# Linear attention and a one-expert mixture on one core: VectorE's order within a block, the release of the row scatter, and the second expert's first loads

## The chip, the core and the metric

The kernel runs on one core of a Trainium2 chip. The metric is the device time of one execution in microseconds (us). The kernel before took 397.58 us in the median of three runs (396.27, 397.58 and 398.49). The profile shown here is of one further execution, which took 397.19 us.

## The reference

Two parts run one after the other. The attention part is a linear recurrence with a decay, over 4 batches, 8 heads, 768 steps and 48 channels; its output is the input of a mixture of 8 experts, in which every one of the 3072 tokens goes to the one expert with the largest logit.

```
for t in range(S):
    cur = einsum('bhd,bhe->bhde', u * k[t], v[t])
    y[t] = einsum('bhd,bhde->bhe', r[t], state + cur)
    state = w[t][..., None] * state + einsum('bhd,bhe->bhde', k[t], v[t])
x = y.transpose(0, 2, 1, 3).reshape(3072, 384)
idx = argmax(x @ w_gate);  gate = softmax(x @ w_gate)[idx]
out[idx == e] = gate * (relu(x[idx == e] @ w1[e]) @ w2[e])
```

## The kernel before

**Attention.** The sequence is cut into 12 chunks of 64 steps, and each chunk into two blocks (two of the four batches each), so there are 24 blocks, numbered n. A call `iteration(n)` holds work of several blocks, since the stages are staggered by hand. The order in which the calls stand in the code is the order on each engine: the lists of TensorE, VectorE, ScalarE, GpSimd and SyncE are written out by hand, and each engine takes its own list in order.

In `iteration(n)` VectorE has: the running product of the decays from the left for block n+2 (`dve_pre`, a scan, and a short reciprocal), the same from the right for block n+1 (`dve_suf`, a scan, L360), the keys of block n+1 times that product (`dve_kh`, L368), and the masked copy of block n (`dve_at`, L373): the scores that TensorE has left in `ap` are copied into `at` where a mask allows. In one iteration of four VectorE also takes the choice of the expert (`gate`) for a group of four blocks, in the next one the place of each row (`place`).

TensorE has in `iteration(n)`: the transposes of the rows of block n-1 (`pe_xT`), the share of the old state (`pe_inter`, L481), the scores from `kh` and `rh` (`pe_a`, L466), the bonus and the transposes of the keys (`pe_kt`), the scores times the values (`pe_av`, L491, which reads `at`), and the state's update (`pe_dp`, L501).

GpSimd has: `rh` (receptance times left product, L395), `rk` (receptance times keys of block n+2, L387), one indirect DMA that scatters 128 finished rows into a table by expert (L604; it is held back until `pe_av(n)`), a tiny memset, and half of the diagonal of `at` (L423). Before `rk`, GpSimd waits for the `kh` of the same iteration, through a dependency added by hand:

```
i = nc.gpsimd.tensor_tensor(out=d["rk"], in0=d["r"], in1=d["k"], op=ALU.mult)
if n > 1:
    after(i, ch["kh"], "one port")
```

SyncE loads the blocks six ahead (L101, L104, L115). All loads of the kernel are issued on SyncE's one queue, in the order of the code.

**From attention to experts.** After the last block the rows of the largest expert (chosen in iteration 18, from the counts so far) are worked on in two portions: `ua` (256 rows, loaded early) and `ub_` (208 rows, loaded when the last scatters have landed). The last eight scatters go out one after the other on GpSimd; the first of them waits for the copy `act_xT(z)` of the last block. `side()` takes one piece of a weight at a time and splits it into a high half (ScalarE, L237) and a low half (VectorE, L239); when a staged piece is used up, `feed()` loads the next one if its expert's number is known. The numbers of experts 2 to 8 in the order of size come from `sort_experts()`; they are read into SyncE's registers (`expert_of`) in one run of seven, behind the load of `ub_`.

**Experts.** For each expert, `mm1` computes eight slabs of the first product (`expand`, L311), the results are split again into two halves (L313, L314), and `contract` or its transposed form makes the second product (L325, L975). TensorE runs nearly without a gap here.

Of the kernel before, what the change touches and what calls it, by code (L numbers as in the profile page):

```python
# [13 lines left out]
ALU = mybir.AluOpType  # L14
# [18 lines left out]
GRP = 4  # L33
# [22 lines left out]
def rwkv_moe_kernel(ctx, tc, rkw, vv, ub, wg, wr, w1, w2, out):  # L56
# [307 lines left out]
    def dve_kh(n):  # L364
        if real(n):
            d = blk[n]
            d["kh"] = work([RP, NSEG, C], F32, "kh")
            ch["kh"] = nc.vector.tensor_tensor(out=d["kh"], in0=d["k"], in1=d["suf"][:, :, 3:SEG], op=ALU.mult)  # L368

    def dve_at(n):  # L370
        if real(n):
# [11 lines left out]
    def pool_rk(n):  # L383
        if real(n):
            d = blk[n]
            d["rk"] = work([RP, NSEG, C], F32, "rk")
            i = nc.gpsimd.tensor_tensor(out=d["rk"], in0=d["r"], in1=d["k"], op=ALU.mult)  # L387
            if n > 1:
                after(i, ch["kh"], "one port")

    def pool_rh(n):
        if real(n):
# [61 lines left out]
    def act_xT(n):  # L454
        if real(n):
            blk[n]["xT"] = t = xtp.tile([P, DM], F32, name="xT", tag="xT")
            ch["xt"] = nc.scalar.activation(t, blk[n]["xp"], AF.Copy)

    def pe_a(n):
        if real(n):  # L460
# [70 lines left out]
    def logit_mm(k):  # L531
        G, at, m = k
        lp = misc("lp")[0:32 * m, 0:P]
        for j in range(3):
            for i in range(m):
                nc.tensor.matmul(lp[32 * i:32 * i + 32], wgt[:, j, :], blk[G * GRP + at + i]["xT"][:, j * P:(j + 1) * P],
                                 start=(j == 0), stop=(j == 2))
        ch["ls"] = ls = sm.tile([P, P], F32, name="ls", tag="ls")[0:32 * m]
        nc.scalar.activation(ls, lp, AF.Copy)

    def logit_tr(k):
        lt = misc("lt")[:, 0:32 * k[2]]
# [161 lines left out]
    def iteration(n):  # L704
        G, i = divmod(n, GRP)
        g = G - 1 if n >= 0 else -1
        whole = (g, 0, GRP)
        if 0 <= n < E // 2:
            prefill(2 * n)
            prefill(2 * n + 1)  # L710
        if n >= 0:
            load(n + 6)
        full = 0 <= g < NG - 1
        if real(n):
            blk[n]["ap"] = psA.tile([P, 4, 256], F32, name="ap", tag="ap")
            pe_xT(n - 1, blk[n]["ap"][:, 1:3, :].rearrange("p a c -> p (a c)"))
            pe_inter(n)
            if full and i == 1:
                logit_tr(whole)
            pe_a(n)  # L720
        dve_scale(n + 1)
        if full and i == 2:
            place(whole)
        act_pend(n + 1)
        act_g(n + 1)
        pool_rh(n + 1)
        dve_suf(n + 1)
        if n == -2:
            pool_rk(0)
        pe_kt(n)  # L730
        act_pad(n + 2)
        dve_kh(n + 1)
        if full and i == 1:
            gate(whole)
        dve_at(n)
        if n == NB - 2:
            side()
        act_kt(n)
        act_ct(n + 1)
        if n > -2:  # L740
            pool_rk(n + 2)
        pe_av(n)
        if n < 2:
            act_diag(n + 1, range(0, H if n < 0 else NQ))
        if n == NB - 2:
            dve_diag(n + 1)
            act_xT(n - 1)
            act_xr(n)
        else:
            act_xr(n)  # L750
            act_xT(n - 1)
        if 2 <= n < NB - 2:
            act_diag(n + 1, range(0, NQ))
        if moved(n) and n < NB - 2:
            scatter(*moved(n), ch["av"])
        if n >= 0:
            pool_diag(n + 1)
        dve_pre(n + 2)
        pe_dp(n)
        if n >= 0:  # L760
            load_v(n + LV)
        if n == FIRST * GRP + 6:
            choose()
            eid[0] = expert_of(first[0:1, 0:1])
            feed()
        if full and i == 0:
            logit_mm(whole)
        if full and i == 1:
            weigh(whole)
            pool_ids(g)  # L770
            rank(whole)
        if n == 3:
            late_constants()
# [65 lines left out]
    with tc.manual_schedule(engines={ET.PE, ET.DVE, ET.Activation, ET.Pool}):  # L839
# [16 lines left out]
        pool_ids(last)  # L856
        pe_av(z)
        logit_mm(ka)
        act_xr(z)
        transpose_rows(ua, 0)  # L860
        pe_xT(z, psA.tile([P, 4, 256], F32, name="xc", tag="ap")[:, 0:2, :].rearrange("p a c -> p (a c)"))
        act_xT(z)
        scatter(last - 1, range(GRP), ch["xt"])
        transpose_rows(ua, 1)
        logit_tr(ka)
        gate(ka)
# [7 lines left out]
        def mm1(u, f):  # L874
            expand(wts[u["e"] % 2], f, u["x"], u["n"], u["hs"])
# [10 lines left out]
        weigh(kb)  # L886
        place(kb)
        scatter(last, (3,))
        mm1(ua, 1)
        side(0)  # L890
        sort_experts()
        check_counts()
        for f in range(2, 8):
            mm1(ua, f)
            side(0)
        actx.close()
        wpb = mctx.enter_context(tc.tile_pool(name="wpb", bufs=1))
        wts.append(weight_tiles(wpb))
# [1 line left out]
        bk["b"].append(mM)  # L900
        while sides and sides[0][1] == 0:
            side(0)
        ub_ = rows_of(HB, HA, 0)
        for e in range(1, E):
            eid[e] = expert_of(order[0:1, e - 1:e])
        feed()
        un = rows_of(CAPS[1], 0, 1)
        tr = [(ub_, j) for j in range(3)]

        def tick():  # L910
# [18 lines left out]
        for e in range(1, E):  # L929
            u = un  # L930
            nth["e"] = e
            while tr:
                trans(*tr.pop(0))
            while sides and sides[0][0] == "split" and sides[0][1] == e:
                side()
            un = rows_of(CAPS[e + 1], 0, e + 1) if e + 1 < E else None
# [258 lines left out]
```

## Time and profile before

| | value |
|---|---|
| median of three runs | 397.58 us |
| the profiled execution | 397.19 us |
| its span (first to last instruction) | 395.5 us |
| around the span | 1.7 us |
| granted TensorE clock, mean | 0.973 |
| busy: TensorE, VectorE, ScalarE, GpSimd | 361.2, 264.2, 195.5, 145.1 us |
| chain that ended last, by engine | TensorE 74%, VectorE 9%, DMA 5%, ScalarE 5%, issue 4% |

A table by stage (the views give the numbers): the attention blocks fill the time up to about 139 us, the change-over some 10 us more, and the experts the rest. "Granted clock" is the share of TensorE's full clock that it was given: 1.00 is 2.4 GHz, 0.50 is 1.2 GHz. In a timeline each line is one group of instructions with start, duration, engine, line of code, operation and the names that it writes and reads; the bracket at its end is the idle time of its engine just before, and what ended it.

### The profile page before, as it was taken

How to read it: one execution, taken by the hardware profiler on the slowest of the kernel's cores; microseconds unless marked ns; L12 is line 12 of the kernel's file. 1: busy time of each engine (PE TensorE's matmuls, PEld its weight loads, DVE VectorE, ACT ScalarE, POOL GpSimd, SP SyncE). 2: the span in 40 equal slices, each digit the busy share in tenths (PEclk: the TensorE clock that was granted, in tenths of full speed). 3: DMA queues.
4: the chain of work that ended last, by engine and by line, in shares of the span. 5: the costliest groups of instructions: out<-in, count | busy, mean ns of one | idle time of the engine just before them, and what ended most of it. 6: DMA issues, size and time to landing. Idle time of an engine off the chain costs nothing.

```text
span 395.5 us, 11603 instructions
## 1 busy us (share of the span) xinstructions
PE 361.2 (91%) x4642; PEld 327.5 (83%) x4642; DVE 264.2 (67%) x451; ACT 195.5 (49%) x516; POOL 145.1 (37%) x195
## 2 busy tenths in 40 slices
PE   7889989797888978989999999999999999999991
PEld 5667767686666757879899899999999999999990
DVE  7788788998989757657565366466476576782410
ACT  4557546655555554445554355464465463761200
POOL 5757477667767728110200040040050171114010
PEclk9699989999999999999999999999999999999998
DMA  7996687777647415398833736466565756821001
GB/s 202 242 257 198 176 256 225 203 211 224 199 120 210 156 43 187 107 295 281 241 110 135 201 97 227 118 188 220 167 181 174 213 120 204 256 78 35 23 19 40
DMA packets 38021, 67.63 MB, mean 171 GB/s; under 512 B 8141, under 2 KB 19714, under 8 KB 37962
## 3 DMA queue, kind: packets, MB, share of 16 engines
q1 hardware_dynamic: 31658, 57.33, 49.5%
q0 software_dynamic: 6304, 9.50, 7.7%
q8 instruction: 38, 0.62, 0.7%
q14 instruction: 21, 0.17, 0.2%
HBM read 55.34 MB, written 11.64 MB: 169 GB/s over the span
## 4 chain that ended last, share of the span: by engine, by line
PE 74%; DVE 9%; DMA 5%; ACT 5%; issue 4%; SPq 1%; POOL 1%; POOLq 0%; DVEq 0%; ACTq 0%
PE N L311 12%; PE N L325 12%; PE cell L311 6%; PE N L975 6%; PE mM L311 6%; PE yp L491 4%; PE cell L975 3%; PE mM L975 3%; PE ap L466 3%; PE yp L481 2%; PE U L501 2%; DMA rkwt<-in_rkw_dram 2%; DVE suf L360 2%; PE ap L529 2%; PE kp L518 2%
## 5 line engine op out<-in xcount | busy, mean ns | idle before, releaser
L275 POOL DMA_INDIRECT out_dram<-ot,gi x16 | 22.2, 1391 | 100.5 <-issue 71.5
L275 POOL DMA_INDIRECT out_dram<-ort,gi x13 | 15.8, 1212 | 68.2 <-DVE ort L330 23.8
L387 POOL TENSOR_TENSOR rk<-rkwt 112x512 f32<-112x512 f32 x24 | 30.5, 1273 | 23.3 <-DVE kh L368 14.3
L239 DVE TENSOR_TENSOR w1l<-wst,w1h 128x512 fp32r<-128x512 f32 x48 | 33.1, 690 | 4.9 <-ACT w1h L237 4.5
L239 DVE TENSOR_TENSOR w2l<-wst,w2h 128x512 fp32r<-128x512 f32 x48 | 32.1, 688 | 6.3 <-ACT w2h L237 6.1
L325 PE MATMUL N<-w2h,hh 128*128 128x384 f32 (+4 forms) x104 | 35.9, 345 | 0.0
L325 PE MATMUL N<-w2l,hh 128*128 128x384 f32 (+4 forms) x104 | 35.0, 337 | 0.0
L325 PE MATMUL N<-w2h,hl 128*128 128x384 f32 (+4 forms) x104 | 35.0, 337 | 0.0
L314 DVE SCALAR_TENSOR_TENSOR hl<-N,hh 128x256 fp32r<-128x256 f32 (+8 forms) x37 | 19.4, 526 | 22.8 <-ACT hh L313 22.8
L237 ACT ACTIVATE w1h<-wst 128x512 fp32r<-128x512 f32 x48 | 30.0, 624 | 5.1 <-DMA wst<-in_w_dram 5.1
L604 POOL DMA_INDIRECT xs<-xr,pi x24 | 24.6, 1025 | 20.6 <-PE yp L491 10.5
L237 ACT ACTIVATE w2h<-wst 128x512 fp32r<-128x512 f32 x48 | 28.4, 625 | 6.4 <-DMA wst<-in_w_dram 6.4
L351 DVE TENSOR_TENSOR_SCAN pre<-rkwt,cell 112x536 f32<-112x536 f32 x24 | 30.3, 1263 | 1.6 <-DMA rkwt<-in_rkw_dram 1.1
L360 DVE TENSOR_TENSOR_SCAN suf<-rkwt,cell 112x536 f32<-112x536 f32 x24 | 30.4, 1266 | 0.5
L313 ACT ACTIVATE hh<-N 128x256 fp32r<-128x256 f32 (+8 forms) x37 | 17.3, 466 | 25.6 <-PE N L311 25.3
L395 POOL TENSOR_TENSOR rh<-rkwt,pre 112x512 f32<-112x512 f32 x24 | 29.7, 1238 | 0.0
L368 DVE TENSOR_TENSOR kh<-rkwt,suf 112x512 f32<-112x512 f32 x24 | 28.8, 1199 | 0.8
L311 PE MATMUL N<-xh,w1h 128*128 128x440 f32 (+6 forms) x84 | 28.8, 343 | 0.0
L311 PE MATMUL N<-xh,w1l 128*128 128x440 f32 (+6 forms) x84 | 28.6, 340 | 0.0
L311 PE MATMUL N<-xl,w1h 128*128 128x440 f32 (+6 forms) x84 | 28.6, 340 | 0.0
L491 PE MATMUL yp<-vt,at 64*64 64x48 f32 x768 | 18.6, 229 | 8.8 <-DVE at L373 8.0
L432 ACT ACTIVATE at<-id,ct 128x64 f32<-128x64 f32 x96 | 25.3, 343 | 0.1
(200 smaller groups left out, 969.2 us busy)
## 6 DMA issues: line engine op xcount, KB each, us to landing
wst<-in_w_dram SPq DMA_DIRECT2D x48, 256.0 KB
wst<-in_w_dram SPq DMA_DIRECT2D x16, 768.0 KB
rkwt<-in_rkw_dram SPq DMA_DIRECT2D x72, 96.0 KB
rkwt<-in_rkw_dram SPq DMA_DIRECT2D x24, 238.0 KB
vt<-in_vv_dram SPq DMA_DIRECT2D x48, 96.0 KB
wck_t<-in_wr_dram SPq DMA_DIRECT2D x6, 768.0 KB
rkwt<-in_rkw_dram SPq DMA_DIRECT2D x12, 224.0 KB
xg<-xs SPq DMA_DIRECT2D x4, 579.0 KB
```

The lines of the kernel that those rows point to most:

```text
L237: nc.scalar.activation(hi, st[:, cs], AF.Copy)
L239: nc.vector.tensor_tensor(out=lo, in0=st[:, cs], in1=hi.bitcast(F32), op=ALU.subtract)
L275: i = nc.gpsimd.indirect_dma_start(out=out[:, :], out_offset=bass.IndirectOffsetOnAxis(ap=t.bitcast(I32)[0:rows.shape[0], q, 1:2], axis=0) ...
L311: nc.tensor.matmul(hp, a, x[p][:, j, :], start=(i == 0), stop=(i == 8))
L325: nc.tensor.matmul(op, a[:, cs], w2v(wt, w, f), start=(i == 0), stop=(i == 23))
L351: nc.vector.tensor_tensor_scan(out=d["pt"][:, 0, 0:NW], data0=d["w"], data1=cell[:RP, 0:1].broadcast_to([RP, NW]), initial=1.0, op0=ALU.mu ...
L360: nc.vector.tensor_tensor_scan(out=suf[:, ::-1], data0=d["w"][:, ::-1], data1=cell[:RP, 0:1].broadcast_to([RP, NW]), initial=1.0, op0=ALU. ...
L368: ch["kh"] = nc.vector.tensor_tensor(out=d["kh"], in0=d["k"], in1=d["suf"][:, :, 3:SEG], op=ALU.mult)
L387: i = nc.gpsimd.tensor_tensor(out=d["rk"], in0=d["r"], in1=d["k"], op=ALU.mult)
L395: nc.gpsimd.tensor_tensor(out=d["rh"], in0=d["r"], in1=d["pre"][:, :, 1:C + 1], op=ALU.mult)
L491: ch["av"] = nc.tensor.matmul(d["yp"][half(b), j, q * D:(q + 1) * D], d["at"][half(h), j, q, :], d["v"][half(h), h, (j * NQ + q) * D:(j * ...
L975: nc.tensor.matmul(pp, w, a, start=(i == 0), stop=(i == 23))
```

## The change

Five things are changed.

1. In `iteration(n)`, VectorE's `kh` of block n+1 comes behind the masked copy of block n instead of ahead of it (not in the last but one iteration). `gate` and `place` come behind the scan `dve_suf`.
2. GpSimd's `rk` no longer waits for `kh`.
3. Four of the last eight scatters are held back until the copy of the logits (`lc`) instead of the copy `act_xT(z)` of the last block, and are issued earlier in GpSimd's list.
4. One more weight piece is split ahead of the second slab and one ahead of the sort; the sort follows behind the third slab; then the number of the second expert is read alone, `feed()` may load its first piece, and only then the rows of `ub_` are asked for. The numbers of the later experts are read one at a time. The check of the counts moves behind the sixth slab.
5. In block 0 TensorE gets three products with zeros behind the scores.

```diff
 def dve_kh(n):
-    ch["kh"] = nc.vector.tensor_tensor(out=d["kh"], in0=d["k"], in1=d["suf"][:, :, 3:SEG], op=ALU.mult)
+    nc.vector.tensor_tensor(out=d["kh"], in0=d["k"], in1=d["suf"][:, :, 3:SEG], op=ALU.mult)
 def pool_rk(n):
-    i = nc.gpsimd.tensor_tensor(out=d["rk"], in0=d["r"], in1=d["k"], op=ALU.mult)
-    if n > 1:
-        after(i, ch["kh"], "one port")
+    nc.gpsimd.tensor_tensor(out=d["rk"], in0=d["r"], in1=d["k"], op=ALU.mult)
...
     pe_a(n)
+    if n == 0:
+        zeros(blk[n]["yp"][:, 1, NQ * D:], 3)
 dve_scale(n + 1)
-if full and i == 2:
-    place(whole)
 act_pend(n + 1)
 act_g(n + 1)
 pool_rh(n + 1)
 dve_suf(n + 1)
+if full and i == 1:
+    gate(whole)
+if full and i == 2:
+    place(whole)
 if n == -2:
     pool_rk(0)
 pe_kt(n)
 act_pad(n + 2)
-dve_kh(n + 1)
-if full and i == 1:
-    gate(whole)
-dve_at(n)
 if n == NB - 2:
+    dve_kh(n + 1)
+    dve_at(n)
     side()
+else:
+    dve_at(n)
+    dve_kh(n + 1)
...
 logit_mm(ka)
+scatter(last - 1, range(GRP), ch["lc"])
 act_xr(z)
 transpose_rows(ua, 0)
 pe_xT(z, ...)
 act_xT(z)
-scatter(last - 1, range(GRP), ch["xt"])
...
 scatter(last, (3,))
+side(0)
 mm1(ua, 1)
 side(0)
+mm1(ua, 2)
+side(0)
 sort_experts()
-check_counts()
-for f in range(2, 8):
+eid[1] = expert_of(order[0:1, 0:1])
+feed()
+ub_ = rows_of(HB, HA, 0)
+for f in range(3, 8):
     mm1(ua, f)
     side(0)
+    if f == 5:
+        check_counts()
...
-ub_ = rows_of(HB, HA, 0)
-for e in range(1, E):
-    eid[e] = expert_of(order[0:1, e - 1:e])
+un = rows_of(CAPS[1], 0, 1)
+eid[2] = expert_of(order[0:1, 1:2])
 feed()
-un = rows_of(CAPS[1], 0, 1)
...
 for e in range(1, E):
     while tr:
         trans(*tr.pop(0))
+    if e + 2 < E:
+        eid[e + 2] = expert_of(order[0:1, e + 1:e + 2])
+        feed()
```

## Rows read from the trace of the kernel before

**Rows 1.** Busy time by stretch: length, then each engine, granted clock, DMA share, GB/s.
```profile
26.00:139.00 113.00, 99.61 (x2745) 79.28 (x2743) 99.05 (x140) 66.14 (x238) 79.08 (x115) 0.97 0.68 197
149.00:193.00 44.00, 38.81 (x261) 36.70 (x260) 28.10 (x71) 21.22 (x49) 12.25 (x20) 0.96 0.71 224
```

**Rows 2.** Groups by line on VectorE, 26 to 139 us: busy, mean ns, idle before.
```profile
L351 DVE TENSOR_TENSOR_SCAN pre<-rkwt,cell 112x536 f32<-112x536 f32 x20 | 25.2, 1262 | 0.3 <-ACT rkwt L399 0.3
L368 DVE TENSOR_TENSOR kh<-rkwt,suf 112x512 f32<-112x512 f32 x20 | 25.1, 1252 | 0.7
L373 DVE COPY_PREDICATED at<-cmask,ap 128x512 f32<-128x512 int32 x21 | 15.5, 737 | 3.8 <-PE ap L466 3.6
L354 DVE RECIPROCAL rkwt<-pre 112x16 f32<-112x16 f32 x20 | 5.1, 256 | 0.7
```

**Rows 3.** The same view, TensorE's and GpSimd's groups, 26 to 139 us.
```profile
L491 PE MATMUL yp<-vt,at 64*64 64x48 f32 x640 | 15.3, 226 | 8.3 <-DVE at L373 7.6 <-issue 0.7
...
L387 POOL TENSOR_TENSOR rk<-rkwt 112x512 f32<-112x512 f32 x19 | 24.2, 1273 | 15.3 <-DVE kh L368 14.3 <-POOL rh L395 0.9
```

**Rows 4.** The instructions of line 368: duration in ns, least, median and most.
```profile
L368 DVE TENSOR_TENSOR kh<-rkwt,suf x24: 692/1118/2255, 6.8 to 138.3; 112x512 f32<-112x512 f32 x24
```

**Rows 5.** Timeline of one period, 104.8 to 111.4 us: start, duration, engine, line.
```profile
104.78 0.68 PE L491 MATMUL yp<-vt,at 64*64 64x48 f32 x32
...
105.77 1.01 POOL L604 DMA_INDIRECT xs<-xr,pi  x1 [0.83 <-PE yp L491]
...
106.84 0.62 POOL L423 TENSOR_TENSOR at<-id,ct 128x256 f32<-128x256 f32 x1
...
107.41 1.18 POOL L395 TENSOR_TENSOR rh<-rkwt,pre 112x512 f32<-112x512 f32 x1
107.45 1.70 DVE L368 TENSOR_TENSOR kh<-rkwt,suf 112x512 f32<-112x512 f32 x1
...
109.82 0.75 DVE L373 COPY_PREDICATED at<-cmask,ap 128x512 f32<-128x512 int32 x1 [0.24 <-PE ap L466]
...
110.73 0.68 PE L491 MATMUL yp<-vt,at 64*64 64x48 f32 x32
```

**Rows 6.** Timeline: two masked copies that follow each other, before scatters begin.
```profile
30.89 0.75 DVE L373 COPY_PREDICATED at<-cmask,ap 128x512 f32<-128x512 int32 x1 [1.10 <-PE ap L466]
...
35.28 0.75 DVE L373 COPY_PREDICATED at<-cmask,ap 128x512 f32<-128x512 int32 x1
```

**Rows 7.** Busy time by stretch, two stretches at half the clock.
```profile
12.70:19.50 6.80, 6.80 (x97) 5.24 (x100) 4.56 (x6) 2.92 (x10) 5.40 (x5) 0.50 1.05 243
...
176.10:180.00 3.90, 3.90 (x20) 3.90 (x21) 3.37 (x8) 2.81 (x7) 0.50 (x1) 0.56 1.00 240
```

**Rows 8.** Timeline of SyncE's DMA issues: loads of block 10 and 22, later loads.
```profile
46.99 1.38 SPq L101 DMA_DIRECT2D rkwt<-in_rkw_dram  x1
...
102.80 0.53 SPq L101 DMA_DIRECT2D rkwt<-in_rkw_dram  x1
...
160.87 0.88 SPq L260 DMA_DIRECT2D xg<-xs  x2
166.22 3.48 SPq L224 DMA_DIRECT2D wst<-in_w_dram  x6
```

**Rows 9.** Timeline of the change-over from attention to experts, 144 to 177 us.
```profile
144.84 0.27 ACT L539 ACTIVATE ls<-lp 96x128 f32<-96x128 f32 x1 [1.45 <-PE lp L536]
...
146.13 0.49 ACT L457 ACTIVATE xT<-xc 128x384 f32<-128x384 f32 x1 [0.37 <-PE xc L529]
...
147.40 1.03 POOL L604 DMA_INDIRECT xs<-xr,pi  x1 [5.47 <-DVE x L302]
...
155.70 0.39 PE L311 MATMUL N<-x,w1l 128*128 128x256 f32 x1 [1.21 <-DVE w1l L239]
...
173.04 0.63 ACT L237 ACTIVATE w1h<-wst 128x512 fp32r<-128x512 f32 x1 [3.12 <-DMA wst<-in_w_dram]
...
176.10 0.48 PE L311 MATMUL cell<-x,w1h 128*128 128x208 f32 x2 [1.79 <-DVE hl L314]
```

More of the change, by code (lines that the diff above doesn't have):

```diff
@@ L456, in act_xT @@
             blk[n]["xT"] = t = xtp.tile([P, DM], F32, name="xT", tag="xT")
-            ch["xt"] = nc.scalar.activation(t, blk[n]["xp"], AF.Copy)
+            nc.scalar.activation(t, blk[n]["xp"], AF.Copy)
     def pe_a(n):
@@ L538, in logit_mm @@
         ch["ls"] = ls = sm.tile([P, P], F32, name="ls", tag="ls")[0:32 * m]
-        nc.scalar.activation(ls, lp, AF.Copy)
+        ch["lc"] = nc.scalar.activation(ls, lp, AF.Copy)
     def logit_tr(k):
```

## Prediction

> **What bounds the kernel now.** I read the table by stretch first. From 26 to 139 us, which holds 20 iterations of attention blocks (VectorE's lines appear 20 times in it), TensorE is busy for 99.6 us of 113 and VectorE for 99.1 [rows 1, 2]: a period is 113 / 20 = 5.65 us, and neither engine is full. So it is a loop between engines that sets the pace, and the waits say which. TensorE's idle time is 13.4 us, and 7.6 us of it stands ahead of the product that reads the masked copy [rows 3]. The masked copy itself waits only 3.6 us for TensorE's scores [rows 2]; mostly it is late because VectorE still has `kh` ahead of it. `kh` lasts 0.69 us at best and 1.25 us in the mean, up to 2.26 [rows 2, 4], and the timeline shows why [rows 5]: it starts at 107.45 beside GpSimd's `rh`, `rh` ends at 107.41 + 1.18 = 108.59, and `kh` ends 0.56 later, at 109.15. It stands still while GpSimd computes. Over 20 iterations that is 25.1 - 20 x 0.69 = 11.3 us of VectorE's time.
>
> The loop is therefore, in the same rows: `av` (ends 105.46), scatter (0.31 later, 1.01 long), diagonal, `rh` to 108.59, `kh` to 109.15, the choice, masked copy to 110.57, next `av` at 110.73: 5.95 us from `av` to `av`. Without scatters the same kernel ran a period in 35.28 - 30.89 = 4.39 us [rows 6].
>
> In the change-over, TensorE is busy for 38.8 of 44 us from 149 to 193 us, at 0.96 of the clock [rows 1]. For the experts after it the change only alters when numbers are read and loads asked for.
>
> **Part 1: order on VectorE, and `rk` free.** No instruction is added or taken away. With `kh` behind the masked copy, `kh` of block n+1 is next needed by the scores of the next iteration, not by `av(n)`, so the loop above is cut. Two loops remain.
>
> VectorE alone: masked copy 0.74, `kh` 0.69, two scans of 1.26 (the second has the same shape and I give it the same), reciprocal 0.26 [rows 2, 4], sum 4.21, and about 0.03 for each of five hand-overs: 4.35 us.
>
> GpSimd's side: after `av` ends, the diagonal ends 2.0 us later (107.46 against 105.46), `rh` at 3.13 [rows 5], and now `rk` stands right behind it with its 1.27 [rows 3] and ends at 4.40. If `kh` must let both pass, it ends at 4.96; left scan, reciprocal, right scan and masked copy follow (3.55 with hand-overs), so the masked copy is done at 8.5 and the `av` after next at 8.5 + 0.16 + 0.68 = 9.35 us. That spans two iterations: 4.7 us each. So even a `kh` that meets `rh` and `rk` each time is no bound above 4.7.
>
> TensorE: 99.6 us busy, less the half-clock stretches within. The mean clock there is 0.97, so 0.03 x 113 = 3.4 us are lost to it [rows 1]; both dips follow on waits of TensorE, and with these gone I let them go. 99.6 - 3.4 = 96.2, or 4.8 us a period. Of the idle 13.4 us, the 7.6 before `av` goes and 5.8 stays (the stops marked issue, the copies of rows). Period (96.2 + 5.8) / 20 = 5.1 us: TensorE is the engine that sets the end here. 113 - 102 = 11 us. I give back 1.5 us, since the port is still met: the price of one meeting is 2.26 - 0.69 = 1.6 us at most [rows 4], and one such on the path is what I allow. **Minus 9.5 us**, with ends at minus 12 and minus 3 (the collisions as in the first rival, and half the waits staying).
>
> `gate` and `place` keep their five short instructions, behind the scan in place of beside `kh`; they fill time in which VectorE would wait for ScalarE and TensorE, so zero, at most 0.3 us a group later. What is behind the waiting masked copy now is `kh` and the left scan; the next to want them are the scores and `rh`, more than 2 us on, so its 3.6 us in all of waiting is covered. Without that cover it is 0.18 us a period.
>
> The Trainium skill, GPSIMD Engine Reference, section Key points, says that GpSimd shares its SBUF interfaces with VectorE and contends with VectorE instructions that have two SBUF inputs. That speaks against freeing `rk`, since `kh` is such an instruction. Rows 5 show the contention in this kernel; by the rule alone, with every `rk` against a `kh`, the time is that of the first rival below.
>
> **Part 2: zeros in block 0.** Between 12.7 and 19.5 us TensorE ran at half its clock and was busy throughout [rows 7], so full clock could save up to 6.8 / 2 = 3.4 us. The three products go into a gap ahead of that stretch and cost nothing there; whether they keep the clock is not shown by any row. If they don't, zero; if they do, loads come next. **Minus 2 us**, ends 0 and minus 3.4.
>
> **Part 3: the last scatters.** The first of eight starts at 147.40, after the copy that ends at 146.62; the logits' copy ends at 145.11 [rows 9], 1.5 us earlier. All eight follow in a row, so the rows of `ub_` can be asked for 1.5 us before 160.87 [rows 8]. Against it, on SyncE's queue the first weight piece of the second expert (half of the 3.5 us of issues at 166.22) now stands ahead of the rows. It is issued while the scatters still land, but its data may be in the rows' way. The 1.2 us stop at 155.70 for a low half [rows 9] also goes, since the split that was late is one step earlier; it is ahead of the wait for the rows, so it does not add. **Minus 1.2 us**, ends plus 1.0 (the issue time of 1.75 not covered, less the gain of one piece) and minus 1.5.
>
> **Part 4: second expert's weights.** SyncE was silent from 160.87 + 0.88 to 166.22 [rows 8]: 4.5 us, the seven reads of expert numbers, about 0.64 each. Only then came the weights; ScalarE's list stood 3.1 us for them at 173.04, the results of `ub_` behind it on the same engine came late, and TensorE waited 1.8 us and then ran 3.9 us at 0.56 of the clock [rows 7, 9], which costs 3.9 x 0.44 = 1.7 us. The number is now known behind the last split ahead of the sort, which was the one late at 155.70; with five short operations and one read (0.64 us) I estimate the first load at 157 to 158, 8 us sooner, so both go: **minus 3.5 us**, ends minus 1.8 (only the wait) and minus 4. The later numbers are read one per expert, each 0.64 us on a queue that waits for free buffers anyway: zero; at worst 0.64 for each of 6, 3.8 us, if pieces came late. The check of counts, five short operations, moves behind work of the same kind: zero.
>
> Sum: -9.5 - 2 - 1.2 - 3.5 = -16.2 us. From the profiled execution, 397.2 (its span is 395.5, 1.7 around it): 381.0 us. The median of the runs is 0.4 above that execution; I leave the forecast at **381 us**.
>
> **Rivals.**
> (a) `kh` meets `rk` each time. If the masked copy is usually early, `kh` pays most of 1.27 us more on VectorE: 4.35 + 1.0 = 5.4 a period with the short operations left out. 20 x (5.65 - 5.4) = 5 us saved in place of 9.5; with 1 us of part 2 and 4 of parts 3 and 4, 397.2 - 10 = 387. For it: `kh` of 2.26 us shows that GpSimd can take two turns in a row. Against it: the loop of 4.7 above.
> (b) The loads set the pace. SyncE issued blocks 10 to 22 in 102.80 - 46.99 = 55.8 us, 4.65 us a block [rows 8], though with little to wait for; if faster blocks stretch that to 5.4 or 5.5, 3 to 5 us are saved, part 2 falls away and 3.5 remain: 390. Against it: at 5.1 us the loads are still the faster.
> (c) Slower. Without the wait, GpSimd can run `rk`, scatter, diagonal, `rh` and the next `rk` with no gap, when `rk` is late (its data, say), and a `kh` that misses its turn stands through all. From the end of the masked copy that is 0.84 to the end of `av`, 2.0 to the end of the diagonal, 1.13 and 1.27 for the two products, 0.56 for `kh` and 3.55 to the end of the next masked copy: 9.4 us for that period, 4.3 more than 5.1. At 16.2 / 4.3, about 4 of 20 iterations, the gain is gone; at 6 in 20 the time is 381 + 26 = 407. For it: that the wait was for just this port. Against it: the scatter waits for `av`, which starts only when the masked copy is done, and `kh` is next on VectorE at that same moment, so the port is normally free for 1 us.
>
> **Chances.** Forecast 0.62, with its own range of 376 to 386; (a) 0.18; (b) 0.10; (c) 0.06; the rest, 0.04, is below 376, where all ends fall on the good side (-12 - 3.4 - 1.5 - 4 = -20.9: 376). The range for 8 in 10 reaches from 375 to 392, which is (b) with only 3 us from part 1 and 1.8 from part 4 (397.2 - 4.8); it leaves out (c) and the far ends. A measurement of this kernel tells about 0.5% (2 us) from no change: faster 0.91, within 0.5% 0.03, slower 0.06.
>
> **What would show it.** `kh` near 0.7 to 1.3 us, but now behind the masked copy; a period of about 5.1 between masked copies; the wait of `av` for the masked copy well below 7.6 us; no clock dip from 50 to 81 us nor near 176; the 22nd masked copy near 127 us; the rows of `ub_` asked for right after the last scatter lands, weights before them. The prediction is wrong if `kh` lasts 2 us or more in the mean, if the period stays over 5.4, or if SyncE's loads get late and the scans wait for them.

## The result, and the profile after

The changed kernel took 394.47 us in the median of 22 executions (389.14 to 400.41), the kernel before 397.69 in 22 beside it (one of them took 1682.52): ratio 0.987 (0.984 to 0.990). Three later comparisons gave 0.983 (0.977 to 0.989), 0.990 (0.986 to 0.994) and 0.978 (0.971 to 0.985); over all four the medians differ by 2.9 to 5.3 us. The forecast was 381, some 16 us less than before. Ratios leave out executions over 1.5% above the fastest of their kernel, so a ratio and the quotient of two medians can differ.

Two profiles of the changed kernel are read here: its first one, a long execution (400.41 us, span 398.7), and that of a later run, again2 (span 388.7). Busy time by stretch in the first, columns as in [rows 1]:

```profile
26.00:139.00 113.00, 104.95 (x2680) 83.71 (x2684) 92.51 (x138) 66.24 (x233) 78.36 (x114) 0.89 0.67 196
139.00:149.00 10.00, 8.44 (x229) 6.83 (x223) 3.95 (x8) 3.78 (x10) 1.53 (x4) 0.75 0.14 43
149.00:193.00 44.00, 38.43 (x267) 36.37 (x266) 28.11 (x72) 22.06 (x52) 11.70 (x20) 0.96 0.67 213
```

and in again2:

```profile
26.00:139.00 113.00, 101.06 (x2873) 80.08 (x2867) 98.21 (x144) 68.87 (x240) 80.37 (x117) 0.98 0.67 195
139.00:149.00 10.00, 9.44 (x84) 7.86 (x76) 6.49 (x22) 6.20 (x19) 7.06 (x13) 1.00 0.38 113
149.00:193.00 44.00, 39.39 (x254) 37.81 (x253) 27.57 (x63) 21.58 (x46) 6.20 (x11) 0.96 0.76 225
```

Against 99.61 us busy at a clock of 0.97 for 2745 products [rows 1], TensorE was busy longer for fewer products in the first profile, at 0.89. Its idle time fell from 13.4 us to 8.1, and in again2 only to 11.9, where 5.8 was forecast. In the first profile, the longest of the 22 executions, the lower clock took back what the idle time gave; what that is worth on average is worked out below from all profiles.

The groups of lines of the first profile, 26 to 139 us, which answer to `kh` and to `av` in [rows 2, 3]:

```profile
L368 DVE TENSOR_TENSOR kh<-rkwt,suf 112x512 f32<-112x512 f32 x20 | 19.7, 984 | 0.0
L489 PE MATMUL yp<-vt,at 64*64 64x48 f32 x640 | 15.7, 235 | 5.6 <-DVE at L373 3.9 <-DVE pre L351 1.7
```

and of again2:

```profile
L368 DVE TENSOR_TENSOR kh<-rkwt,suf 112x512 f32<-112x512 f32 x20 | 24.4, 1219 | 0.0
L489 PE MATMUL yp<-vt,at 64*64 64x48 f32 x692 | 15.5, 223 | 1.8 <-DVE at L373 1.8
```

`av` waited 7.6 us for the masked copy before; now 3.9 and 1.8. One period in the first profile's timeline (answers to [rows 5]):

```profile
78.69 0.71 DVE L373 COPY_PREDICATED at<-cmask,ap 128x512 f32<-128x512 int32 x1
...
79.30 1.19 DVE L368 TENSOR_TENSOR kh<-rkwt,suf 112x512 f32<-112x512 f32 x1
...
79.46 0.78 PE L489 MATMUL yp<-vt,at 64*64 64x48 f32 x32 [0.28 <-DVE at L373]
...
80.53 1.01 POOL L602 DMA_INDIRECT xs<-xr,pi  x1 [0.60 <-PE yp L489]
...
82.18 1.19 POOL L393 TENSOR_TENSOR rh<-rkwt,pre 112x512 f32<-112x512 f32 x1
...
83.32 1.27 POOL L387 TENSOR_TENSOR rk<-rkwt 112x512 f32<-112x512 f32 x1
...
84.20 0.74 DVE L373 COPY_PREDICATED at<-cmask,ap 128x512 f32<-128x512 int32 x1 [0.24 <-ACT ex L564]
```

`kh` stands behind the masked copy, beside `av`, and `rk` directly behind `rh`: the loop is cut as the prediction drew it.

Where the time then went, in the same profile. First, a late copy:

```profile
113.28 0.62 POOL L421 TENSOR_TENSOR at<-id,ct 128x256 f32<-128x256 f32 x1
...
113.71 2.57 DVE L623 TENSOR_SCALAR pen<-key,ks 1x8 f32<-1x8 f32 x1
...
113.85 1.18 POOL L393 TENSOR_TENSOR rh<-rkwt,pre 112x512 f32<-112x512 f32 x1
...
114.99 1.26 POOL L387 TENSOR_TENSOR rk<-rkwt 112x512 f32<-112x512 f32 x1
...
117.39 0.69 DVE L373 COPY_PREDICATED at<-cmask,ap 128x512 f32<-128x512 int32 x1
...
118.13 1.16 PE L489 MATMUL yp<-vt,at 64*64 64x48 f32 x30 [2.67 <-DVE at L373]
```

`pen`, eight numbers of the expert's choice, lasts 2.57 us, to just after the end of `rk` at 116.25; the masked copy is late and TensorE stands 2.67 us. Behind that stop, and behind one of 1.62 us marked issue at 126.96, TensorE runs at half its clock, 1.2 GHz (windows of the first profile; the clock is the third number from the end):

```profile
116.70:123.40 6.70, 5.27 (x115) 4.54 (x115) 4.65 (x6) 2.19 (x7) 3.77 (x5) 0.50 0.86 271
130.30:140.50 10.20, 10.20 (x175) 8.21 (x174) 5.81 (x12) 3.69 (x14) 2.94 (x5) 0.50 0.18 58
```

The second of these stretches is busy throughout. The 22nd masked copy, which was forecast near 127 us, starts at 131.54 (133.13 before, 127.58 in again2). Second, in the change-over, ScalarE's line of the first profile and, behind it, SyncE's and TensorE's of again2:

```profile
160.51 0.38 ACT L313 ACTIVATE hh<-N 128x256 fp32r<-128x256 f32 x1 [3.74 <-remote]
```

```profile
149.60 0.98 POOL L602 DMA_INDIRECT xs<-xr,pi  x1 [0.23 <-ACT w2h L237]
...
151.25 1.40 SPq L224 DMA_DIRECT2D wst<-in_w_dram  x3
...
155.03 0.87 SPq L260 DMA_DIRECT2D xg<-xs  x2
...
159.72 0.37 PE L300 MATMUL N<-ident,xg 104*128 104x104 f32 x2 [3.70 <-DMA xg<-xs]
```

The second expert's weights are asked for 14.1 us after the last masked copy (137.13), not 23.8 as in [rows 8], and ScalarE's list no longer waits for them; TensorE stands 3.70 us for the rows.

### The profile page after: what moved, and what is told of

Its sections match the earlier page's. It is cut to its first block, busy times and chain, and to the rows that moved or that the text cites. A ratio compares the mean times of both kernels' runs of the same rounds, so it can differ in the third digit from the quotient of the medians.

```text
span 398.7 us, 11609 instructions
## 1 busy us (share of the span) xinstructions
PE 367.8 (92%) x4644; PEld 332.8 (83%) x4645; DVE 259.1 (65%) x451; ACT 196.5 (49%) x516; POOL 144.0 (36%) x195
## 4 chain that ended last, share of the span: by engine, by line
PE 76%; DVE 6%; issue 5%; DMA 3%; ACT 3%; POOL 2%; SPq 2%; another core or an unknown queue 1%; POOLq 0%; DVEq 0%; ACTq 0%
PE N L325 13%; PE N L311 13%; PE cell L311 7%; PE mM L311 6%; PE N L986 6%; PE cell L986 3%; PE mM L986 3%; PE yp L489 3%; PE ap L464 3%; PE U L499 2%; PE yp L479 2%; PE N L300 2%; PE wrm L142 2%; PE ap L527 2%; PE kp L516 2%
## 5 line engine op out<-in xcount | busy, mean ns | idle before, releaser
L313 ACT ACTIVATE hh<-N 128x256 fp32r<-128x256 f32 (+8 forms) x37 | 17.3, 467 | 27.3 <-PE N L311 22.5
L373 DVE COPY_PREDICATED at<-cmask,ap 128x512 f32<-128x512 int32 x24 | 17.6, 735 | 19.2 <-PE ap L464 13.1
L393 POOL TENSOR_TENSOR rh<-rkwt,pre 112x512 f32<-112x512 f32 x24 | 28.9, 1203 | 1.4 <-DVE pre L351 0.9
```

The source lines that it names most:

```text
L393: nc.gpsimd.tensor_tensor(out=d["rh"], in0=d["r"], in1=d["pre"][:, :, 1:C + 1], op=ALU.mult)
```

## The experiments

**The two halves, and `rk` apart** (one comparison; the kernel before 396.02 us). `order_only` has parts 1 and 2, as the prediction numbers them, alone (the hunks of the diff up to `iteration`), `head_only` parts 3 and 4 alone (those behind it), `rk_waits` is the changed kernel with GpSimd waiting for `kh` again, `again` the changed kernel.

```diff
 # rk_waits, against the changed kernel (pool_rk)
-nc.gpsimd.tensor_tensor(out=d["rk"], in0=d["r"], in1=d["k"], op=ALU.mult)
+i = nc.gpsimd.tensor_tensor(out=d["rk"], in0=d["r"], in1=d["k"], op=ALU.mult)
+if n > 1:
+    after(i, ch["kh"], "one port")
```

Expected of order_only: 

> Only the order on VectorE, the free product of GpSimd and the zeros of block 0; scatters, sort and weights of the change-over as before. Theory A: 392 to 395, since the loss of clock comes from the attention blocks, and 2 to 3.5 us above the changed kernel, which is what the change-over is worth. Theory B: 386 to 389, faster than the changed kernel by about 4. Theory C: 394 to 396.

Expected of head_only: 

> Only the change-over (scatters released earlier, one split more ahead of the sort, second expert's number and first piece ahead of the rows); attention blocks as before. Theory A and C: 393 to 395.5, 2 to 4 us below the kernel before (the forecast was 4.7). Theory B: 399 to 402, slower than before.

Expected of rk_waits: 

> The changed kernel with one thing put back: GpSimd's second product waits for the keys' product, which now stands behind the masked copy. Theory A: the loop masked copy, keys' product, second product, scatter gets longer than the free one, so 0 to 3 us slower than the changed kernel. Theory C: 3 or more faster than the changed kernel, keys' product 0.7 to 0.8 us in the mean.

Expected of again: 

> The changed kernel once more, to have a profile beside the others. Theory A (the shorter periods are real, but TensorE, which now has no slack, falls to half its clock more often and gives most of it back): about 391 to 395 us, at least 8 of the 17 periods from block 5 to block 22 at 5.1 us or less, and the time lower the higher the granted clock. Theory B (the attention blocks are some 9 us faster, the change-over some 4 us slower, since ScalarE stops there for 3.7 us in the profile): a stop of over 3 us of ScalarE again between the second and third slab. Theory C (the product that no longer waits blocks the keys' product at the port): keys' product over 1.2 us in the mean.

Measured: order_only 392.92 us, ratio 0.979 (0.971 to 0.987); head_only 394.74, 0.996 (0.992 to 1.000); rk_waits 392.09, 0.977 (0.969 to 0.984); again 390.95, 0.983 (0.977 to 0.989). Parts 3 and 4 give 1.6 us (0 to 3.2), where 4.7 were forecast. Freeing `rk` adds nothing that these times resolve once `kh` is behind the masked copy. order_only and head_only came out as their theory A; rk_waits stands 1.1 us above `again` in the medians and below it in the ratios, so its A is not shown and its C, 3 us or more below, did not come. `again` lies at the lower edge of its A, with 7 periods of 5.1 us or less where at least 8 were expected, without the stop of ScalarE of its B, and with a mean `kh` of 1.15 us against its C. In order_only one stop was followed by that profile's longest stretch at half clock, with TensorE busy throughout; first the `kh` of that period, then the stop, then the window:

```profile
33.41 3.21 DVE L368 TENSOR_TENSOR kh<-rkwt,suf 112x512 f32<-112x512 f32 x1
```

```profile
39.95 0.57 PE L516 MATMUL kp<-ident,kh 112*128 112x112 f32 x4 [0.94 <-DVE oh L562]
```

```profile
40.70:54.20 13.50, 13.50 (x259) 11.28 (x259) 8.02 (x14) 6.27 (x21) 6.65 (x9) 0.50 0.74 198
```

The stop is a wait for `oh`, a part of `gate`, which stands behind this `kh` and the scans on VectorE; `kh` ran beside `rh`, the free `rk` and the diagonal. In the new order such a `kh` (2.9 to 3.2 us, at 33 to 35 us) is in eight of the nine profiles with `rk` free and in none of the three in which `rk` waits, and a stop of TensorE for `oh` of 0.66 to 1.42 us follows in six of the eight. So freeing `rk` has a price there.

**`rk` free in the old order**, against the kernel before (399.28 us in this and the next three runs):

```diff
-if n > 1:
-    after(i, ch["kh"], "one port")
```

> The kernel before with only part 2 of the change: rk no longer waits for kh, VectorE's order is the old one with kh ahead of the masked copy. Theory A (the wait kept rk from standing between rh and kh, and kh is on the path in the old order): kh passes rk as well as rh wherever rk's data is there, kh about 2.3 us long in the mean in place of 1.12, the period grows by up to 1.2 us in 20 iterations: 400 to 420. Theory B (GpSimd and VectorE take turns, so it doesn't matter who is next): kh stays near 1.1 us in the mean and the time is that of the kernel before within 2 us, 394 to 398.

Measured 413.39 us, ratio 1.035 (1.030 to 1.040): theory A. Its timeline:

```profile
105.30 1.19 POOL L393 TENSOR_TENSOR rh<-rkwt,pre 112x512 f32<-112x512 f32 x1
...
105.53 2.73 DVE L368 TENSOR_TENSOR kh<-rkwt,suf 112x512 f32<-112x512 f32 x1
...
106.45 1.26 POOL L387 TENSOR_TENSOR rk<-rkwt 112x512 f32<-112x512 f32 x1
...
108.19 0.71 DVE L373 COPY_PREDICATED at<-cmask,ap 128x512 f32<-128x512 int32 x1
```

`kh` now stands through `rh` and `rk`, with the masked copy behind it. The two edits of part 1 belong together: the wait was worth 14 us in the old order and nothing that the times resolve in the new one. The mean of `kh` was 1.80 us from 26 to 139 us, less than the 2.3 of the expectation.

**Stops taken away one by one.** `pen_late` computes `pen` at the sort; `rows_first` asks for the rows of `ub_` ahead of the first weight piece; `hot` gives TensorE 38 more products of zeros (its expectation counts 40, but block 2 had its two before).

```diff
 # pen_late: in choose(), and at the head of sort_experts()
-nc.vector.tensor_scalar(out=pen, in0=key, scalar1=ks[:, 0:1], scalar2=-FAR, op0=ALU.is_equal, op1=ALU.mult)
+ch["c"] = (key, ks)
...
+k1, ks1 = ch["c"]
+nc.vector.tensor_scalar(out=pen, in0=k1, scalar1=ks1[:, 0:1], scalar2=-FAR, op0=ALU.is_equal, op1=ALU.mult)
 # rows_first
 eid[1] = expert_of(order[0:1, 0:1])
-feed()
 ub_ = rows_of(HB, HA, 0)
+feed()
 # hot
-ZEROS = {0: 4, 1: 4, 2: 2, 22: 6}
+ZEROS = {0: 4, 1: 4, **{n: 2 for n in range(2, 22)}, 22: 6}
```

Expected of pen_late: 

> The changed kernel, with one 1x8 operation of the expert's choice (pen, 2.57 us long in two profiles of the changed kernel while GpSimd ran three operations in a row) moved from the loop to the sort of the experts, where GpSimd only issues scatters. Theory A (TensorE's rare long stops cost their own length and then a stretch at half clock): the stop of 2.7 to 3.0 us near 113 us goes, and the half-clock stretch behind it; the masked copy of block 19 comes 5 to 5.5 us after that of block 18 in place of 7.6; about 2 us for the stop and 1.7 to 3.4 for the clock, so 387 to 389 where the changed kernel has 391 to 394. Theory B (the attention's gain is small because VectorE and GpSimd collide wherever they meet, pen is only the one that shows): the next VectorE operation with two inputs, kh, stands in its place, the period stays near 7, and the time is that of the changed kernel within 1 us.

Expected of rows_first: 

> The changed kernel with the first weight piece of the second expert asked for behind the rows of ub_ instead of ahead of them; the number is still read early. Theory A (the piece's data is in the way of the last scatters, which land 4.3 us after the last was issued in place of 2.8 to 3.1, and the rows wait for that): rows asked for about 3.0 us after the last scatter, TensorE's stop ahead of the rows' transposes falls from 2.2 to 2.8 us to about 1, and the half-clock stretch of 3.4 us behind it goes: 1.3 + 1.7 = 3 us less than the changed kernel, 388 to 391. Theory B (the rows are bound by the scatters' own row of eight and nothing else): the stop stays above 2 us, time as the changed kernel. Theory C (the piece is then late): ScalarE's list waits for a weight for 1 us or more near 169 us as it did before the change, plus 1 to 2 us.

Expected of hot: 

> The changed kernel with two more products of zeros (128x320 columns, about 0.14 us each at full clock) on TensorE in each of blocks 2 to 21. Theory A (what is missing of the attention's gain is TensorE's clock, which falls behind a stop and stays down for 3 to 17 us because the attention's products are small): the half-clock stretches between 26 and 139 us become shorter, the mean granted clock rises from about 0.972 to 0.985 or more, and that pays for the 20 x 0.28 = 5.6 us that the products cost at most: 388 to 394. Theory B (the clock doesn't hang on what TensorE does there): granted clock as before, about 0.97, and the time 3 to 6 us above the changed kernel, 396 to 399.

Measured: pen_late 392.81 us, 0.983 (0.977 to 0.990); rows_first 394.00, 0.986 (0.980 to 0.992); hot 397.63, 0.998 (0.994 to 1.002). In pen_late's profile block 19's copy follows 4.83 us after block 18's (7.62 in the changed kernel's first profile) and no half-clock stretch is left ahead of the change-over:

```profile
110.98 0.73 DVE L373 COPY_PREDICATED at<-cmask,ap 128x512 f32<-128x512 int32 x1 [1.06 <-PE ap L464]
...
115.81 0.75 DVE L373 COPY_PREDICATED at<-cmask,ap 128x512 f32<-128x512 int32 x1 [0.32 <-PE ap L464]
```

Yet its time is not below the changed kernel's beyond the scatter of the runs: a miss for the size. Nor did every stop of TensorE bring half clock there: behind one of 1.62 us at 123.9 the clock stayed full. rows_first can't be judged by its stop, since ScalarE stood 3.7 us in that execution and the rows were in time; its time, where 388 to 391 was expected, is a miss. In hot theory A is a miss and B came out: the mean clock of its executions was 0.976 (rows_first 0.973, pen_late 0.980, before 0.973), and the products cost more than they gave.

**Parts of the change-over, and all edits together** (the kernel before 395.44 us). `head_rows` is head_only with the rows ahead of the piece, `scatter_only` is part 3 alone, `best` is rk_waits with pen_late and rows_first.

```diff
 # scatter_only, against the kernel before
 logit_mm(ka)
+scatter(last - 1, range(GRP), ch["lc"])
...
-scatter(last - 1, range(GRP), ch["xt"])
```

Expected of again2: 

> The changed kernel once more, as the measure for the other three. Theory A (the loop is as short as forecast while TensorE has its full clock, and rare stops of 1.1 us or more put it at half): between 26 and 139 us the wait of av for the masked copy is 2 to 4.5 us in place of 7.6, undisturbed periods are 4.7 to 5.2 us, and the granted clock of that stretch says how much of it is left: 0.94 or lower with the last masked copy at 140 us or later, 0.99 or more with it at 135 to 138 us. Theory B (the period itself is only 0.2 us shorter): last masked copy at 140 us or later even at a clock of 0.99. Time 391 to 395 if the kernel before has 396 to 398.

Expected of best: 

> The changed kernel with three edits together: rk waits for kh again (behind the masked copy now), pen is computed at the sort of the experts, and the first weight piece is asked for behind the rows of ub_. Theory A (what is lost is a few stops and the clock behind them): no stop of over 2 us between 26 and 139 us, none over 1.3 us ahead of the rows, clock 0.975 or more in the mean, 3 to 6 us less than the changed kernel: 385 to 390. Theory B (the stops move on, the next instruction block or the next late copy puts TensorE at half clock in their place): as the changed kernel within 1.5 us.

Expected of head_rows: 

> The kernel before with parts 3 and 4 of the change, but the first weight piece of the second expert asked for behind the rows of ub_. Theory A (the piece delays the landing of the last scatters and so the rows): the rows are asked for about 17.2 us or less after the last masked copy has started (17.7 with the piece ahead, 18.4 before the change), TensorE's stop ahead of the rows' transposes is below 2 us in place of 2.64, and 1 to 3 us less than with the piece ahead: ratio to the kernel before 0.988 to 0.993. Theory B (the train of eight scatters alone sets the rows): 17.7 us and a stop of 2.6 us again, ratio 0.996. Theory C (the piece now comes too late): ScalarE waits 1 us or more for a weight near 169 us, ratio 0.996 to 1.0.

Expected of scatter_only: 

> The kernel before with part 3 of the change alone: the first four of the last eight scatters wait for the copy of the logits. Theory A (part 3 as it was forecast): the rows are asked for 1 to 1.5 us sooner, 17 us after the last masked copy has started in place of 18.4, and 0.5 to 1.2 us of time are gained. Theory B (TensorE doesn't stand on the rows alone; its 1.2 us stop for a low half and ScalarE's 3.1 us for the second expert's weights stand before and behind them): the rows come sooner and the time is that of the kernel before within 0.5 us.

Measured: again2 390.19 us, 0.990 (0.986 to 0.994); best 385.55, 0.976 (0.970 to 0.982); head_rows 392.18, 0.992 (0.988 to 0.995); scatter_only 395.10, 1.001 (0.997 to 1.005). TensorE's stop ahead of the rows, in head_only and then in head_rows:

```profile
163.83 0.58 PE L300 MATMUL N<-ident,xg 104*128 104x104 f32 x2 [2.64 <-DMA xg<-xs]
```

```profile
166.55 0.40 PE L300 MATMUL N<-ident,xg 104*128 104x104 f32 x2 [1.83 <-DMA xg<-xs]
```

The piece in the rows' way was worth about 0.8 us of the stop in these two executions, and the rest of the stop is another's. Part 3 alone gave nothing, and the rows came only 0.4 us sooner (17.99 us after the last masked copy in place of 18.43), nearest to theory B. again2 has a wait of `av` below the range of its A, and its last masked copy at 137.13 speaks against B. best came out at the time of its A, but not for A's reason: its profile has the stops that A excludes, 2.05 us at 119.4 and 1.60 ahead of the rows.

**Does TensorE set the pace now?** `hot_old` has the 38 products of zeros in the old order; `two_edits` is best with `rk` free; best_again and again3 stand beside them (the kernel before 397.55 us).

Expected of hot_old: 

> The kernel before with the same 40 products of zeros as in the run hot (two in each of blocks 2 to 21). Theory A (in the old order the pace was the loop over kh and the masked copy, and TensorE had 13 us to spare between 26 and 139 us; in the new order it has 8 to 12 us, in short stops, and sets the pace): the 5.6 us of products fall into the wait of av for the masked copy, which shrinks from 7.6 to below 5 us, and the time is at most 2 us above the kernel before, where they cost the changed kernel about 4. Theory B (TensorE's work was on the path in the old order as well): 4 us or more above the kernel before, ratio 1.01 or more.

Expected of two_edits: 

> The changed kernel with pen computed at the sort and the first weight piece behind the rows; rk stays free. Theory A (those two take away the stops that cost most, freeing rk is worth nothing either way): within 1.5 us of best_again and 3 us or more below again3. Theory B (freeing rk costs, since kh stands up to 3.2 us behind rh and rk): 2 us or more above best_again.

Expected of best_again: 

> The three edits together once more (rk waits for kh behind the masked copy, pen at the sort, the piece behind the rows). If the run best was no accident: 4 to 5 us below again3, ratio to the kernel before 0.970 to 0.980.

Expected of again3: 

> The changed kernel, as the measure for the other three: ratio to the kernel before 0.983 to 0.990. Where its profile shows no half-clock stretch between 26 and 139 us the last masked copy starts at 135 to 138 us; with 10 us or more of them, at 140 us or later.

Measured: hot_old 399.30 us, 1.005 (1.001 to 1.009); two_edits 387.37, 0.973 (0.969 to 0.978); best_again 390.83, 0.985 (0.980 to 0.991); again3 394.65, 0.978 (0.971 to 0.985). The waits of TensorE in hot_old, 26 to 139 us (total, times, longest):

```profile
PE yp L491 <- DVE at L373: 5.2, 9, 1.2
```

The products fall in part into that wait (7.6 in [rows 3]) and cost 2.0 us; in the new order, where hot's ratio stands 0.8 to 2 points above the changed kernel's of the other comparisons, 3 to 8. Over the 14 periods measured below, 28 of them add about 5 us to TensorE's busy time in either order, so all 38 would cost 6 to 7 us with no wait to fall into. This is theory A in kind.

The kernels with pen at the sort and the rows first were 3.8 to 7.3 us below the changed kernel beside them, in the medians of three pairs. The ratios bear this out for best and two_edits, but best_again's 0.985 is not below again3's 0.978, so its expectation of 0.970 to 0.980 is a miss, as again3's of 0.983 or more is. two_edits is the fastest against its kernel before, 2.7% below (2.2 to 3.1). It differs from best_again only in that `rk` is free and lies 3.5 us below it, outside the 1.5 us of its theory A; but best and best_again, the same kernel, differ as much in their ratios. Which of the edits carries the gain is not told apart.

**Why the earlier scatters bring no earlier rows.** `piece_late` is scatter_only with the first expert's last weight piece held back until the rows are asked for:

```diff
 # feed()
+if ch.get("hold") and todo[0] == (0, 3):
+    return
...
+ch["hold"] = True
...
 ub_ = rows_of(HB, HA, 0)
+ch["hold"] = False
+feed()
+while sides and sides[0][1] == 0:
+    side(0)
```

> scatter_only with the last piece of the first expert's weights asked for behind the rows of ub_, and not about 11 us after the last masked copy has started, in the middle of the train of eight scatters. Theory A (the scatters behind that piece land only when its data is through): the rows are asked for 3.0 us or less after the last scatter was issued, 15 to 16.5 us after the last masked copy has started, in place of 4.5 and 17.9. Theory B (the train's own landing is that slow): 17.5 us or more again. The second product then waits for that piece, so the whole is 2 to 6 us slower than scatter_only; its time says nothing about the question.

The last scatter and SyncE's issues in scatter_only, then in piece_late:

```profile
149.62 0.39 SPq L227 DMA_DIRECT2D wst<-in_w_dram  x1
...
151.02 0.97 POOL L604 DMA_INDIRECT xs<-xr,pi  x1 [0.23 <-ACT w1h L237]
...
156.55 0.87 SPq L260 DMA_DIRECT2D xg<-xs  x2
```

```profile
150.13 0.97 POOL L604 DMA_INDIRECT xs<-xr,pi  x1 [0.23 <-ACT w1h L237]
...
152.93 0.87 SPq L260 DMA_DIRECT2D xg<-xs  x2
...
154.07 0.41 SPq L227 DMA_DIRECT2D wst<-in_w_dram  x1
```

From the end of the last scatter's issue to the asking for rows: 156.55 - 151.99 = 4.6 us with the piece in the middle of the train, 152.93 - 151.10 = 1.8 without. Theory A, in one profile of each. The other nine profiles without ScalarE's stop (last section) agree: in all of them the rows are asked for 6.9 to 8.3 us after that piece, whether the last scatter's issue ended 2.8 or 4.6 us before. The one execution of piece_late took 390.81 us beside 394.99 for the kernel before, not 2 to 6 us more than scatter_only as was expected: ScalarE waited 1.74 us for the late piece and TensorE 0.80 behind it.

## Why the prediction was wrong

**Part 1, the loop: right in kind; its clock: the step that failed.** The step reads "both dips follow on waits of TensorE, and with these gone I let them go". The waits for the masked copy shrank, the dips stayed. Over 14 periods, from the masked copy of block 4 to that of block 18 (start to start), with the time at half clock in between (without hot, hot_old and rk_free_old, whose work or waits differ):

| order | kernel: us (of it at half clock) |
|---|---|
| old | scatter_only 79.4 (0), piece_late 79.6 (0), head_rows 80.1 (6.8), before 80.5 (6.8), head_only 81.5 (3.4) |
| new, none | first profile 71.7, again 74.0, best 74.3, pen_late 76.8 |
| new, some | best_again 78.0 (6.8), two_edits 78.2 (13.7), again2 78.3 (3.4), rows_first 78.6 (7.0), order_only 78.8 (13.7), again3 79.4 (10.2), rk_waits 81.0 (17.1) |

The loop did get shorter: of the 17 periods from block 5 to block 22, none is 5.1 us or less in any of the seven profiles with the old order, and 4 to 11 are in each of the twelve with the new one. Without half clock the 14 periods of the new order take 71.7 / 14 = 5.12 us each at best, the 5.1 that was forecast, and 5.30 in the mean, against 5.73 for the old five. With half-clock stretches it is 5.6 to 5.8, and the mean of all eleven, 5.51, is above the 5.4 that the prediction named as a sign of being wrong.

What the sum had wrong shows when the 14 periods are taken apart (means of the five and of the eleven profiles): TensorE's busy time, less half of its time at half clock, is 68.3 us in the old order and 67.9 in the new; its idle time 10.2 and 6.0; the loss to half clock (half of that time) 1.7 and 3.3. The forecast, taken for 14 of 20 periods, has 5.3 us less idle time and 2.4 us less loss to the clock. The idle time fell by 4.2, so the mechanism held and that term was a little large; the loss to the clock rose by 1.6 in place of falling. Seven of the eleven profiles have a half-clock stretch in these periods, and three of the old five; the profile that the forecast was made from, with 6.8 us, had twice the mean of the five.

In the old order the wait for the masked copy takes up most of such a stretch: 6.8 us at half clock, a loss of 3.4, go with 0.8 us more (80.3 against 79.5). In the new order each us at half clock goes with 0.35 us over the eleven profiles, where 0.5 is the full price. The cover of the old order has an end: the last five periods, 26.3 to 27.3 us in the old order with 3.4 us or less at half clock, took 32.0 with 11.7 in head_rows; in the new order 24.9 to 26.6 without half clock and 30.1 to 34.8 with 10 us or more. hot_old and hot show the same cover for added work. Over whole executions the difference between the two orders is small: each 0.01 of mean clock goes with 2.5 us within the changed kernel's 22 executions (correlation -0.84) and with 2.3 within the 62 of the kernel before in the three later comparisons (-0.80). There the changed kernel's mean granted clock was 0.972, 0.977 and 0.974, that of the kernel before 0.980, 0.978 and 0.976. Of the forecast's 16.2 us, 3.4 here, 2 in part 2 and 1.7 in part 4 were clock to be won back: 7.1. The mean clock did not rise, so none of it shows.

That a stop stands ahead of each stretch is shown: in all nineteen profiles every half-clock stretch that begins between 20 and 180 us has a stop of TensorE of 0.66 us or more in the 5 us ahead of it, `pen`'s, the rows' and those of order_only among them. That taking such a stop away takes the stretch away is not: pen_late's profile lost both, but again2 and again3, with `pen` in its place, have no stretch there either, and stops as long as 1.65 us (again3, 125.9 us) pass without one. Many of the stops are marked issue, which names no wait, and no part of the change is aimed at those. What decides whether a stop brings a stretch, and whether that lasts 3.4 or 17 us, busy throughout in both, is open.

From the first masked copy to the last the five profiles of the old order take 128.3 us in the mean (125.3 to 132.0), eleven of the new 126.4 (123.0 to 131.1): 1.9 us of the 11.5 of parts 1 and 2. The profiled executions of the new order were on average 1.9 us longer than the medians of their runs, those of the old order 0.6, so some 3 us is nearer to the usual execution. The 22nd masked copy near 127 us did not follow from the sum: 133.13 - 11.5 is 121.6.

**Part 2: small, and not shown.** Half clock between 12 and 20 us stands in two of seven profiles without the zeros (before, rk_free_old) and in none of twelve with them, too few to tell. The profile before happened to have it; -2 us could be the size for such executions only.

**Part 3: wrong.** The scatters start and end 1.5 to 1.9 us sooner, as forecast, but the last of them land behind a weight piece that SyncE asks for in the middle of their train, and the rows wait for the landing. The prediction looked at the queue that issues and not at what else is in flight. The Trainium skill, DMA: Bandwidth & Descriptors, section Queues, rings and completion order, says that each DMA engine takes packets in turn from the queues that have work for it. piece_late is in keeping with that, with 1.8 us in place of 4.6; that the packets took turns no run here shows.

**Part 4: half.** The wait for weights of 3.12 us, the stop of 1.79 and the half clock behind it [rows 9, 7] are gone. "Where a stall goes, what is late next" was asked and not answered: TensorE now reaches the rows sooner and stands there 2.2 to 3.7 us (0.81 before), with a half-clock stretch of 3.4 us behind it in again, again2, head_only and rk_waits. From the last masked copy to the end: 253.1, 252.3 and 252.5 us without parts 3 and 4 or with part 3 alone, 250.5, 250.6, 251.6 and 250.8 with both (profiles without ScalarE's stop): 1.7 us of 4.7. With the rows ahead of the piece it is 250.2 (head_rows) and 249.2 (best).

1.9 + 1.7 = 3.6 us, and the medians show 2.9 to 5.3.

**The rivals.** (a) `kh` did meet `rk` (up to 3.2 us in again2), but behind the masked copy it is mostly off the path: rk_waits is no faster beyond the scatter. The exception is the period with `gate`, where the late `oh` stops TensorE. (b) No scan waited for loads to speak of. (c) is what happens in the old order, as rk_free_old shows; in the new one the masked copy goes first.

## What to carry to other kernels

When a wait of the busiest engine goes, the cover of its clock goes with it: count a half-clock stretch near its full price from then on, and don't book its disappearance as gain unless the stops ahead of it are named one by one. Two edits that look independent (an order, and a wait that protected the old order) are to be tried apart. For a chain that ends in a DMA's landing, ask what other transfers are in flight when it lands, not only when it is issued.

## What was not expected of the hardware

- A VectorE operation on eight numbers (`pen`, 1x8) lasted 2.57 us where GpSimd ran three operations back to back; 2.57 in `again`, 2.60 in `hot`, and 0.21 to 0.72 us in the other profiles. The Trainium skill, GPSIMD Engine Reference, section Key points, names VectorE instructions with two SBUF inputs as ones that contend with GpSimd. `pen` takes a row and a scalar from SBUF, while three neighbours with one input, 113.27 to 113.8 us in the same profile, kept their 0.14 to 0.16 us beside GpSimd's diagonal. The trace agrees with the rule, and a size of eight numbers was no protection.
- ScalarE stood 3.4 to 3.7 us at one place of its list (L313, 3.74 above) with nothing that the profile names, and TensorE 4.3 to 4.6 behind it in most of these. It is in nine of nineteen profiles: in the first of the changed kernel, in all eight of two comparisons and in none of the nine of the other three, nor in that of the kernel before, and in both orders, so it is not the change's; in `hot` the part marked remote was 2.3 us. The changed kernel's medians are 394.47 and 394.65 us in the comparisons in which its profile has the stop and 390.95 and 390.19 where it has not; those of the kernel before move less, 397.69 and 397.55 against 396.02 and 395.44. The cause of the stop was not found.
- Stretches at half clock lasted 3.4 to 17.1 us with TensorE busy throughout (one of 20.5 in best, busy for 19.3), as in rk_waits, where one of 17 us followed a stop of 1.84:

```profile
45.90:62.90 17.00, 17.00 (x310) 14.28 (x308) 12.24 (x17) 8.37 (x28) 10.67 (x13) 0.50 0.75 209
```
